# Strassen's scheme for probabilities times values in the attention of a Conformer block

## Chip, core and metric

The kernel runs on one core of one Trainium2 chip. The metric is the device time of one execution in microseconds; the time of a kernel is the median of several runs. A profiled execution is another, single execution with the hardware profiler on.

## What is computed

One Conformer block for 2 sequences of 4,000 tokens of 512 features (bf16): feed-forward with half a residual, attention with one head of 512 features, a convolution module with a norm over all tokens, a second feed-forward and a last layer norm.

```python
h = _layernorm(x)
x1 = x + 0.5 * (_silu(h @ w_ff1_a) @ w_ff1_b)          # 512 -> 2048 -> 512
h = _layernorm(x1)
q, k, v = h @ w_q, h @ w_k, h @ w_v
p = _softmax(einsum('btd,bsd->bts', q, k) * D ** -0.5)
x2 = x1 + einsum('bts,bsd->btd', p, v) @ w_o
h = _layernorm(x2) @ w_pw1                              # 512 -> 1024
h = h[..., :D] * _sigmoid(h[..., D:])
dc = depthwise convolution of h over 3 tokens, then a norm over all tokens
x3 = x2 + _silu(dc) @ w_pw2
h = _layernorm(x3)
return _layernorm(x3 + 0.5 * (_silu(h @ w_ff2_a) @ w_ff2_b))
```

## The kernel before

**Tiling.** The 8,000 tokens are cut into 16 chunks, 8 per sequence: seven of 508 tokens (four tiles of 127) and one of 444. Everything of one chunk is done by the four engines in a hand-written order of emission: `S.op` and `S.dma` put an instruction into the queue of its engine and work out its waits from the buffers that it reads and writes; each engine then goes through its own queue in order. `after(n, fn)` puts work off by n steps (a step, `tick`, is one key tile in attention), `lags` is a list of products held back. SyncE (SP) issues nearly all DMAs, one at a time in the order of emission, so a DMA that waits for its data holds all DMAs behind it.

**Stages.** Feed-forward one runs to about 410 us of the span, attention to about 1475, the end of the convolution with its norm to about 1503, feed-forward two and the last norm to the end. The work of the convolution module for chunk g-1 and g-2 is laid between the key tiles of attention chunk g. Both feed-forward stages already use Strassen's scheme in most chunks (`ff_quad`, L1006), whose weight sums are made by `ff_weights` and, for feed-forward two, by `wa_sums` (L982) in attention chunk 2 from weights (`raw`) that are loaded in chunk 1.

**Attention.** Weights are folded beforehand: `M` takes the place of w_q and w_k, `Wvo` that of w_v and w_o, so both scores and the second product work on the layer-normed tokens h themselves. For one sequence, `hT` holds h with features on the partitions (for the scores), `h` holds it with tokens on the partitions (`keys` in the profile). `attention` (L1276) goes through 16 query chunks g and, in each, through 32 key tiles kt: 31 of 128 keys and a tail of 32. For each key tile:

- scores: four matmuls (`s` <- `work`,`keys`, one per 128 features) into one of four PSUM banks;
- `act` (L663): ScalarE exponentiates into a ring of 8 tiles `P`;
- VectorE adds the tile in f32 to `acc` (L1312), the sums of the softmax;
- `values` (L1320), four tiles later: four matmuls (`y` <- `work`,`keys`) of h's four blocks of 128 features times `P`, accumulated over the whole chunk in four further banks `Yb`.

After the last key tile `split_sums` and `sums_by_query` (L1402, L1417) turn `acc` into a reciprocal per query, by a DMA transpose; `copy_o` (L1431) takes `Yb` out of PSUM by ScalarE and VectorE (L660), and `project` (L1437), in steps 6 to 9 of the next chunk, multiplies by `Wvo` and adds to the tokens (`residual`, L872). Then `projected` starts `ln_job` (L753): statistics (L726), four norms by VectorE (L745), and behind each a DMA transpose (L671) from SP, whose results feed the first convolution product, `conv_b` and `conv_a` (L1471, L1481), at key tiles 22 and 27 of the same and 3 and 8 of the following chunk; `taps_beside` (L1528) does the depthwise part on VectorE.

For the next chunk, `fetch_queries` (a DMA transpose from `keysd` in DRAM) is at key tiles 7 to 10 and `q_group`, four matmuls by `M` each, at 14, 16, 18 and 20 (in chunk 1 at 3, 4, 14, 16, with the fetch in chunk 0), with copies by ScalarE and VectorE in turn (L1222). Chunk 0 begins while feed-forward one's last chunk ends; SP then still loads most key tiles of the first sequence (`load_rest`). In chunks 7 and 8 the keys of the second sequence are loaded over those of the first, key tile by key tile (`key_tile`, L1392). Conv results go to DRAM and are fetched again by `fetch_conv` (L1574): pieces 0 to 2 at the end of attention, pieces 3 and 4 in the first steps of feed-forward two (hook at L1990), where `swish` (L1642) on ScalarE reads them.

If a bound on the scores fails (`fold_weights`, L1673, against `SCORE_LIMIT`), a second program with row maxima runs instead (`any_score`); with these inputs it does not.

Of the kernel before, what the change touches and what calls it, by code (L numbers as in the profile page):

```python
# [25 lines left out]
HALF = 64  # L26
HC, HD, HF = CHUNK // 2, D // 2, FC // 2
# [6 lines left out]
SCORE_LIMIT = 60.0  # L34
# [224 lines left out]
class Conformer:  # L259
    LN_SLOTS = 4  # L260

    TAIL_AT = 18
# [28 lines left out]
    def memory(self):  # L291
        nc = self.nc
        self.XR = Region(nc, "xt", (self.SLOTS + 1) * 4096)
        self.bxs = [[Buf("x%d.%d" % (n, t)) for t in range(TPC)] for n in range(self.SLOTS + 1)]
# [13 lines left out]
        self.raw = E.view(16384, DC * F).rearrange("p (c f) -> p c f", c=DC)  # L308
        self.b_raw = [E.buf("raw", 16384 + n * 4096, 4096) for n in range(DC)]
# [37 lines left out]
        def take(n):  # L347
# [23 lines left out]
        oWvo = take(4096)  # L371
        self.M = C.view(oM, 2048).rearrange("p (c f) -> p c f", c=DC)
# [7 lines left out]
        self.b_OTr = [Buf("OTr") for cc in range(DC)]  # L380

# [20 lines left out]
        GW = CHUNK + 4  # L402

# [22 lines left out]
        homes = ((C, oQ1), (E, 28672))  # L426
# [10 lines left out]
                   [(C, oOT + k * 1024) for k in range(4)] + [(E, k * 1024) for k in range(4)]),  # L437
# [104 lines left out]
    def slot(self, c, n=SLOTS):  # L542

        return self.SLOTS if c == TCB - 1 else self.SLOTS - n + (c - (c >= TCB)) % n
# [157 lines left out]
    def load_x(self, c):  # L702
        if c < NCK:
            self.place(c, self.slot(c))
# [48 lines left out]
    def ln_job(self, c, kind, eng="DVE", plan=(1, 1, 2, 2, 3, 4, 5, 5, 6, 6), slot=None, pe=None):  # L753
# [5 lines left out]
        def tile(ti):  # L759
            if kind == "key":  # L760
                self.ln_norm(c, sl, ti, self.h2[c % 2][ti][0:TILE, :], self.b_h2[c % 2][ti], eng)
# [85 lines left out]

    def store_keys(self, c):
# [7 lines left out]
        h2, b_h2 = self.h2[c % 2], self.b_h2[c % 2]  # L856
        put(self.pieces(c, flat, self.h2c[c % 2]), b_h2, [self.b_keysd[c]] + (self.b_keyst if c == TCB - 1 else []))
# [124 lines left out]
    def wa_sums(self, w, b_w, n):  # L982
# [7 lines left out]
        for h in range(2):  # L990
            self.S.op("DVE", lambda e, h=h: e.tensor_tensor(out=out[:, h], in0=x[:, h], in1=y[:, h], op=op),
                      reads=rd + b_w, writes=wr)

# [218 lines left out]
    def q_group(self, b, qc, dc):  # L1212
# [8 lines left out]
        if dc % 2:  # L1221
            self.S.op("DVE", lambda e: e.tensor_copy(self.qT[s][:, dc, 0:W], ps[:, 0:W]),  # L1222
                      reads=[b_ps], writes=[self.b_qT[s][dc]])
        else:
            self.act(self.qT[s][:, dc, 0:W], ps[:, 0:W], AF.Copy, [b_ps], [self.b_qT[s][dc]])
# [50 lines left out]
    def attention(self, old, hook, done):  # L1276
        S = self.S
        LAG = 4
        for g in range(NCK):
            b, qc = divmod(g, TCB)  # L1280
            s, W = qc % 2, width(g)
            if self.any_score:
                if qc == 0:
                    self.pop(len(self.lags))
                    if not b:
                        self.load_rest(2 * KT, KT * 2)
                    if b:
                        for kt in range(KT):
                            self.key_tile(1, kt)
                self.row_max(qc)  # L1290
            for kt in range(KT):
                kc, kj = divmod(kt, TPC)
# [3 lines left out]
                if kt < KT - 1:  # L1296
                    ps, b_ps = self.sbank()
                    p = self.nxt("Pa", self.NP - 1) if self.any_score else self.nxt("P", self.NP)
                    for cc in range(DC):
                        self.mm(ps[:, 0:W], self.hT[kc][:, kj, cc, :], self.qT[s][:, cc, 0:W],  # L1300
                                cc == 0, cc == DC - 1 and not self.any_score,
                                [self.b_hT[kc][kj], self.b_qT[s][cc]], b_ps)
                    if self.any_score:
                        self.mm(ps[:, 0:W], self.one3, self.m3[:, 0:W], False, True,
                                [self.b_one3] + self.b_m3, b_ps)
# [776 lines left out]
```

## Time and profile before

| | us |
|---|---|
| median of 3 runs (1947.73 to 1954.67) | 1950.62 |
| the profiled execution | 1952.81 |
| its span | 1948.8 |
| PE, DVE, ACT busy in the span | 1934.8, 1426.1, 1003.0 |
| PE, DVE, ACT busy from 60 to 450 us | 388.1, 312.8, 274.1 |
| from one chunk of attention to the next (518.0 to 585.9) | 67.9 |

The span lies within the profiled execution's own time; the difference of 4 us is before its first and after its last instruction. The span's lines in the profile are named by engine: PE is TensorE (PEld its weight loads), DVE VectorE, ACT ScalarE, POOL GpSimd, SP the engine that issues DMAs (SPq its queue). A group is written as line, engine, operation, output <- inputs by tile name, shapes, count, busy time, mean of one, idle time before it and what ended that. Matmuls overlap in the record: a busy PE need not be at its peak, so a matmul's price is read from the distance of two starts.

### The profile page before, as it was taken

How to read it: one execution, taken by the hardware profiler on the slowest of the kernel's cores; microseconds unless marked ns; L12 is line 12 of the kernel's file. 1: busy time of each engine (PE TensorE's matmuls, PEld its weight loads, DVE VectorE, ACT ScalarE, POOL GpSimd, SP SyncE). 2: the span in 40 equal slices, each digit the busy share in tenths (PEclk: the TensorE clock that was granted, in tenths of full speed). 3: DMA queues.
4: the chain of work that ended last, by engine and by line, in shares of the span. 5: the costliest groups of instructions: out<-in, count | busy, mean ns of one | idle time of the engine just before them, and what ended most of it. 6: DMA issues, size and time to landing. Idle time of an engine off the chain costs nothing.

```text
span 1948.8 us, 31991 instructions
## 1 busy us (share of the span) xinstructions
PE 1934.8 (99%) x12626; PEld 1258.4 (65%) x12626; DVE 1426.1 (73%) x2743; ACT 1003.0 (51%) x1726; POOL 108.4 (6%) x235
## 2 busy tenths in 40 slices
PE   9999999999999999999999999999999999999998
PEld 5899999954444444445444444444455789999997
DVE  7788888745566667666766666676687888888885
ACT  5677777743333333333333333333337678777774
POOL 1000000000000000000000000000002000000000
PEclk9999999999999999999999999999999999999999
DMA  8233344264121221114531212211134322222211
GB/s 183 72 87 86 80 114 106 69 159 133 26 52 25 49 53 49 37 44 101 135 61 41 59 28 47 55 49 35 44 108 127 75 76 65 78 53 55 63 40 44
DMA packets 270443, 139.59 MB, mean 72 GB/s; under 512 B 202568, under 2 KB 261643, under 8 KB 270287
## 3 DMA queue, kind: packets, MB, share of 16 engines
q1 hardware_dynamic: 269609, 137.14, 28.4%
q8 instruction: 101, 1.65, 0.3%
q14 instruction: 55, 0.45, 0.1%
q10 hardware_dynamic: 678, 0.34, 0.1%
HBM read 53.26 MB, written 39.20 MB: 47 GB/s over the span
## 4 chain that ended last, share of the span: by engine, by line
PE 95%; SPq 2%; DVE 1%; DMA 1%; issue 0%; ACT 0%; POOL 0%; POOLq 0%; DVEq 0%
PE y L613 48%; PE s L613 47%; SPq L671 1%; SPq L667 1%; DVE work L726 0%; SPq L706 0%; DMA work<-in_dw_dram 0%; DMA work<-keysd 0%; DMA work<-work 0%; DVE xt L872 0%; SPq L675 0%; DVE work L905 0%; DVE xt L745 0%; PE y L641 0%; DVE sums L1003 0%
## 5 line engine op out<-in xcount | busy, mean ns | idle before, releaser
L613 PE MATMUL y<-work,keys 128*127 128x256 bf16 (+2 forms) x3904 | 739.9, 324 | 0.0
L663 ACT ACTIVATE work<-s 128x508 bf16<-128x508 f32 (+2 forms) x543 | 317.9, 586 | 642.8 <-PE s L613 640.4
L613 PEld LDWEIGHTS y<-work,keys 128*128 128x128 bf16 (+1 forms) x3904 | 408.2, 117 | 232.1 <-DVE work L660 0.6
L1312 DVE TENSOR_TENSOR work<-work 128x508 f32<-128x508 f32 (+1 forms) x480 | 324.1, 675 | 260.7 <-ACT work L663 257.9
L613 PE MATMUL s<-work,keys 128*128 128x508 bf16 (+2 forms) x2240 | 506.0, 356 | 0.0
L613 PEld LDWEIGHTS s<-work,keys 128*128 128x128 bf16 (+1 forms) x2240 | 195.7, 97 | 228.7 <-ACT work L663 5.8
L663 ACT ACTIVATE keys<-s 128x508 bf16<-128x508 f32 (+1 forms) x281 | 163.7, 585 | 176.8 <-PE s L613 114.7
L613 PE MATMUL y<-wff,keys 128*127 128x256 bf16 (+3 forms) x1592 | 210.0, 281 | 0.2 <-DVE xt L959 0.2
L726 DVE BATCH_NORM_STATS2 work<-xt 127x6 f32<-127x512 bf16 x311 | 196.5, 680 | 3.5 <-DMA xt<-in_x_dram 3.4
L613 PE MATMUL s<-sums 128*128 128x254 bf16 x1296 | 194.4, 273 | 2.2 <-DVE s L1038 2.2
L613 PE MATMUL s<-work,wff 128*128 128x508 bf16 (+4 forms) x884 | 188.5, 353 | 0.7 <-ACT work L663 0.4
L613 PEld LDWEIGHTS y<-wff,keys 128*127 128x127 bf16 (+1 forms) x1592 | 176.7, 136 | 18.1 <-issue 7.1
L918 DVE TENSOR_TENSOR keys<-keys 128x1016 bf16<-128x1016 bf16 x240 | 160.2, 680 | 4.2 <-ACT keys L663 2.1
L613 PE MATMUL s<-work 128*127 128x512 bf16 (+4 forms) x569 | 143.7, 378 | 5.2 <-DMA work<-in_dw_dram 2.1
L613 PEld LDWEIGHTS s<-sums 128*128 128x128 bf16 x1296 | 126.8, 98 | 20.5 <-DVE s L1038 2.4
L733 POOL TENSOR_TENSOR work<-work 127x4 f32<-127x4 f32 (+1 forms) x76 | 77.2, 1015 | 1046.8 <-DVE work L731 1046.8
L613 PE MATMUL y<-work,wff 128*128 128x254 bf16 (+1 forms) x892 | 135.3, 274 | 0.0
L613 PEld LDWEIGHTS s<-work,wff 128*128 128x128 bf16 x884 | 81.1, 98 | 81.5 <-issue 4.9
L663 ACT ACTIVATE work<-xt,work 127x512 bf16<-127x512 bf16 x148 | 119.6, 810 | 17.2 <-DVE work L738 16.9
L613 PEld LDWEIGHTS s<-work 128*127 128x127 bf16 (+2 forms) x569 | 66.3, 119 | 63.0 <-issue 3.4
L1038 DVE TENSOR_TENSOR s<-s,sums 128x508 f32<-128x508 f32 x108 | 74.9, 693 | 34.0 <-PE s L613 21.2
L613 PEld LDWEIGHTS y<-work,wff 128*128 128x128 bf16 x892 | 87.0, 98 | 10.4 <-ACT keys L663 0.5
(130 smaller groups left out, 1607.7 us busy)
## 6 DMA issues: line engine op xcount, KB each, us to landing
xd<-xt SPq DMA_DIRECT2D x28, 448.0 KB, 3.0
xt<-xd SPq DMA_DIRECT2D x28, 448.0 KB, 3.6
keys<-keysd SPq DMA_DIRECT2D x62, 128.0 KB, 2.3
out_dram<-xt SPq DMA_DIRECT2D x14, 448.0 KB, 3.2
dcvd<-wff SPq DMA_DIRECT2D x48, 127.0 KB, 1.8
keys<-dcvd SPq DMA_DIRECT2D x12, 508.0 KB, 3.7
xt<-in_x_dram SPq DMA_DIRECT2D x13, 448.0 KB, 4.6
wff<-in_w_ff_b_dram SPq DMA_DIRECT2D x8, 512.0 KB, 7.7
```

The costliest lines, as they stand in the source:

```text
L613: self.S.op("PE", lambda e: e.matmul(out, lhsT, rhs, start=start, stop=stop, **kw), reads=reads, writes=[bank], inc=stop if inc is None el ...
L663: return self.S.op("ACT", lambda e: e.activation(out, in_, func, **kw), reads=reads, writes=writes)
L667: return self.S.dma(eng, k, lambda e: e.dma_start(dst, src), reads=reads, writes=writes)
L671: return self.S.dma("SP", k, lambda e: e.dma_start_transpose(dst, src), reads=reads, writes=writes)
L726: self.S.op("DVE", lambda e: e.bn_stats(self.st[sl][:, ti, 0:6], x), reads=[b_x], writes=[self.b_st[sl][ti]])
L733: S.op("POOL", lambda e: e.tensor_tensor(out=self.rs[sl][:, 0:n], in0=self.mv[sl][:, 0:n, 1], in1=self.neghalf[0:TILE, 0:n], op=ALU.pow), ...
L918: self.S.op("DVE", lambda e, out=out, x=x, y=y, op=op: e.tensor_tensor(out=out, in0=x, in1=y, op=op), reads=rd, writes=wr)
L1038: S.op("DVE", lambda e: e.tensor_tensor(out=out, in0=h[:, W], in1=m5, op=ALU.add), reads=[b_h, b_m5], writes=[b_out])
L1312: S.op("DVE", lambda e, p=p: e.tensor_tensor(out=acc, in0=acc, in1=self.P[p][:, 0:W], op=ALU.add), reads=[self.b_P[p], self.b_acc[s]], wri ...
```

## The change

In chunks 0 to 14 the product of probabilities and values of key tiles 0 to 29 goes by pairs of key tiles in Winograd's form of Strassen's scheme: with a pair's 256 keys as two halves, the queries as two halves of 254, and the features as two halves of 256, seven products of half width (two matmuls each) stand in place of eight matmuls of full width. Tile 30 and the tail stay plain, and so does chunk 15.

- `exp_pair` writes each exponential as two pieces into two rings (`R`, `T`); `pair_sums` makes five sums and differences in bf16 and adds two of them to `acc`, on VectorE; where 31 tiles were added in f32, one operation per pair and one for tile 30 are left.
- `pv`: products 1, 2, 5, 6, 7 run from key tile 7 on, each in a PSUM bank of its own; products 3 and 4 and the last pairs' remainder run in key tiles 0 to 6 of the next chunk, in banks that `pv_join` has emptied; scores have three banks in place of four. `pv_join` puts the seven together with six operations on VectorE and three on ScalarE.
- The forms of h that the scheme needs (three sums kept beside h in `VF`, two differences in place) are made by VectorE: for the first sequence in chunk 0 (`v_here`), for the second ahead, in chunks 0 and 1, through DRAM (`v_ahead`), and loaded in chunks 7 and 8 (`v_back`). Chunk 15 loads 30 plain key tiles again at key tiles 7 to 14.
- All query copies and the four norms of `ln_job` before the convolution go to ScalarE; the projection moves to key tiles 9 to 12, the norms to 16 and 17, convolution pairs to 20 and 24 and, in the next chunk, 3 and 14; the query fetch moves from key tile 7 to 9, the tail's scores from 18 to 22.
- The weight sums of feed-forward two are made in the last chunk of feed-forward one (`wa_ahead`, through DRAM), and read again at the first step of feed-forward two (`wa_back`), ahead of `fetch_conv(3)`.
- `SCORE_LIMIT` falls from 60 to 1.5; the first program is still the one that runs.

The core of the diff (moved buffers, joins, forms and the fallback's copy of the old loop are left out):

```diff
+PAIRS = 15
-SCORE_LIMIT = 60.0
+SCORE_LIMIT = 1.5
-    TAIL_AT = 18
+    TAIL_AT = 22
...
+    def exp_pair(self, g, kt, ps, b_ps):
+        i, odd = divmod(kt, 2)
+        n, m, _, _ = self.p_home(g, i)
+        W, hw = width(g), width(g) // 2
+        oTo, oR, oTe = self.offs
+        lo, hi = ((oR + n * 4 * HC, oTe + m * 2 * HC), (oTo + m * 2 * HC, oR + n * 4 * HC + 2 * HC))[odd]
+        t = self.E.view(lo, hw)
+        out = bass.AP(tensor=t.tensor, offset=t.offset, ap=[list(t.ap[0]), [(hi - lo) // 2, 2], [1, hw]])
+        self.act(out, ps[:, 0:W].rearrange("p (h k) -> p h k", h=2), AF.Exp, [b_ps],
+                 [self.b_R[n] if not odd else self.b_R2[n], self.b_T[odd][m]], scale=SCALE)
+    def pair_sums(self, g, j, step):
+        S, s, W = self.S, g % TCB % 2, width(g)
+        hw = W // 2
+        i, n = 2 * j, min(2, PAIRS - 2 * j)
+        r, m, ft, b_f = self.p_home(g, i)
+        R = self.Rt[:, r:r + n, :, 0:hw]
+        a11, a22 = R[:, :, 0], R[:, :, 1]
+        te, to = [t[:, m:m + n, 0:hw] for t in self.Tt]
+        b_te, b_to = [b[m:m + n] for b in self.b_T]
+        b_11, b_22 = self.b_R[r:r + n], self.b_R2[r:r + n]
+        f = [ft[:, k, 0:n, 0:hw] for k in range(3)]
+        if step < 5:
+            out, x, y, op, rd, wr = ((f[0], a11, to, ALU.add, b_11 + b_to, [b_f[0]]),
+                                     (f[1], te, a22, ALU.add, b_te + b_22, [b_f[1]]),
+                                     (f[2], a11, a22, ALU.add, b_11 + b_22, [b_f[2]]),
+                                     (te, te, a11, ALU.subtract, b_te + b_11, b_te),
+                                     (to, to, a22, ALU.subtract, b_to + b_22, b_to))[step]
+            S.op("DVE", lambda e: e.tensor_tensor(out=out, in0=x, in1=y, op=op), reads=rd, writes=wr)
+            return
...
+    PV_BANK = {1: 4, 6: 5, 7: 6, 5: 7, 3: 7, 2: 3, 4: 3}
+    def pv(self, g, n, pairs):
+        hw = width(g) // 2
+        ps, b_ps = self.bank(self.PV_BANK[n])
+        for i in pairs:
+            r, m, ft, b_f = self.p_home(g, i)
+            R, T, f = self.Rt[:, r], [t[:, m] for t in self.Tt], ft[:, :, i % 2]
+            he, ho, v = self.h[2 * i], self.h[2 * i + 1], self.VF[i]
+            b_he, b_ho, b_v = self.b_h[2 * i], self.b_h[2 * i + 1], self.b_VF[i]
+            form, b_1, mv, b_2 = {1: (v[:, 0], b_v, f[:, 2], b_f[2]), 2: (he[:, 0:HD], b_he, f[:, 1], b_f[1]),
+                                  3: (he[:, HD:D], b_he, R[:, 0], self.b_R[r]), 4: (ho[:, 0:HD], b_ho, R[:, 1], self.b_R2[r]),
+                                  5: (ho[:, HD:D], b_ho, f[:, 0], b_f[0]), 6: (v[:, 1], b_v, T[0], self.b_T[0][m]),
+                                  7: (v[:, 2], b_v, T[1], self.b_T[1][m])}[n]
+            for u in range(2):
+                self.mm(ps[:, u * hw:(u + 1) * hw], form[:, u * 128:(u + 1) * 128], mv[:, 0:hw],
+                        i == 0 and u == 0 and n not in (3, 4), u == 1, [b_1, b_2], b_ps, skip_group_check=True)
...
+    def units(self, g, kt, fast, lag, group):
+        end = PAIRS // 2 - 1
+        if lag:
+            o = g - 1
+            if kt == 0:
+                self.pv(o, 1, group(end))
+                self.pv_rest(o, 0, (2, 5))
+                self.pv(o, 2, group(end + 1))
+                self.pv(o, 5, group(end + 1))
+                self.pv_rest(o, 1, (2, 5))
+                self.pv_join(o, 0)
+                self.split_sums(o)
+                self.sums_by_query(o % TCB % 2)
+            elif kt == 1:
+                for n in (6, 7):
+                    self.pv(o, n, group(end))
+                for n in (1, 6, 7):
+                    self.pv(o, n, group(end + 1))
+                self.pv_rest(o, 0, (7, 6))
+                self.pv_rest(o, 1, (7, 6))
+                self.pv_join(o, 1)
+                self.pv_join(o, 2)
+            elif kt < 7:
+                m = (kt - 2) * 6
+                for n in range(m, m + 6):
+                    self.pv(o, 3 if n >= PAIRS else 4, [n % PAIRS])
+                if kt == 2:
+                    self.pv_join(o, 3)
+                    self.pv_join(o, 4)
+                if kt == 4:
+                    self.pv_join(o, 5)
+                if kt == 6:
+                    self.pv_join(o, 6)
+            elif 9 <= kt < 9 + TPC:
+                self.project(o, kt - 9)
+        if not fast:
+            return
+        j, r = divmod(kt - 7, 4)
+        if 0 <= j <= end:
+            order = ((1, 6), (7,), (2,), (5,)) if j == 0 else ((2, 5), (1,), (6,), (7,))
+            for n in order[r]:
+                self.pv(g, n, group(j))
+        j, r = divmod(kt - 4, 4)
+        if 0 <= j <= end:
+            for n in ((0, 1), (2, 3, 4), (5,), (6,))[r]:
+                self.pair_sums(g, j, n)
+        if kt == KT - 2:
+            for n in (0, 1):
+                self.pair_sums(g, end + 1, n)
+        if kt == KT - 1:
+            for n in (2, 3, 4, 5):
+                self.pair_sums(g, end + 1, n)
+            self.sum_plain(g, KT - 2, self.P30, self.b_P30)
...
+    def keys_swap(self, g, kt, G):
+        at = g * KT + kt
+        if g == 0:
+            j, r = divmod(kt - 3, 3)
+            if 0 <= j <= G and r < 2:
+                for n in range(2 * r, 2 * r + 2):
+                    self.v_here(j, n)
+            if kt in (26, 27):
+                self.v_rest(kt - 26)
+        if g < 2:
+            for j, lo in enumerate((6, 12, 18, 24, 32, 35, 41, 44)):
+                if at in (lo, lo + 3, lo + 4, lo + 6):
+                    for n in {0: (0,), 3: (1, 2), 4: (3, 4), 6: (5,)}[at - lo]:
+                        self.v_ahead(j, n)
+        if TCB - 1 <= g <= TCB:
+            at -= (TCB - 1) * KT
+            for k in range(KT):
+                if (6 + k * (2 * KT - 12) // KT if k < KT - 1 else KT + 6) == at:
+                    self.key_queries(1, k)
+            for j in range(G + 1):
+                if at == min(4 * j + 13, KT + 3 + j - G):
+                    self.v_back(j, True)
+                if at == KT + 5 + j:
+                    self.v_back(j, False)
+            if at in (KT + 3, KT + 4):
+                self.key_values(1, KT - 2 + at - KT - 3)
+            if at in (KT + 14, KT + 15):
+                self.v_rest(at - KT - 14)
...
+    def wa_back(self):
+        dst = self.E.view(0, 8192).rearrange("p (m f) -> p m f", m=8)
+        for half in range(2):
+            n = HF * 128 // 2
+            self.load(dst[:, :, half * n:(half + 1) * n], self.wsd[half].rearrange("p (m f) -> p m f", m=8),
+                      self.b_wsum, reads=[self.b_wsd[half]])
...
+        here, there = ((22, 27), (3, 8)) if any_score else ((20, 24), (3, 14))
         def att_hook(g, kt):
             if g == 0 and kt == 8:
                 self.load(self.Wp1, i["w_pw1"].rearrange("(c p) f -> p c f", p=128), [self.b_Wp1])
-            if kt in (22, 27) and (0 <= g - 1 < tail or g - 1 == tail and (22, 27).index(kt) < self.KEEP):
-                pair(g - 1, (22, 27).index(kt))
-            if 0 <= g - 2 < tail and kt in (3, 8):
-                pair(g - 2, 2 + (3, 8).index(kt))
+            if kt in here and (0 <= g - 1 < tail or g - 1 == tail and here.index(kt) < self.KEEP):
+                pair(g - 1, here.index(kt))
+            if 0 <= g - 2 < tail and kt in there:
+                pair(g - 2, 2 + there.index(kt))
             if g == 0 and self.rest:
                 self.load_rest(FC + kt, 3)
-            if kt == 12:
-                self.get_x(g, self.slot(g, 3))
-            if g == 1 and kt < DC:
-                self.load(self.raw[:, kt, :], i["w_ff2_a"].rearrange("(c p) f -> p c f", p=128)[:, kt, :], [self.b_raw[kt]])
-            if g == 2 and kt in (2, 5, 12, 15):
-                self.wa_sums(self.raw, self.b_raw, (2, 5, 15, 12).index(kt))
+            if kt == (12 if any_score else 22):
+                self.get_x(g, self.slot(g, 0, 2))
+            if g and kt == 9 and not any_score:
+                self.ln_job(g - 1, "in", "ACT", (2, 3, 4, 5, 6, 7, 8, 8, 9, 9), slot=0)
+                self.after(7, lambda: self.put_x(g - 1))
             if g == NCK - 1:
                 if 8 <= kt < 20 and not any_score:
                     self.tap_matrix(kt - 8)
                 if kt in (22, 25, 28):
                     self.fetch_conv((kt - 22) // 3)
-                if kt in (2, 5, 8):
-                    self.get_x((kt - 2) // 3, self.slot((kt - 2) // 3))
+                if kt in (12, 15, 18):
+                    self.get_x(kt // 3 - 4, self.slot(kt // 3 - 4, 2))
...
+                if c == 0 and f == 0:
+                    self.wa_back()
                 if c == 0 and f < 2:
                     self.fetch_conv(3 + f)
```

More of the change, by code (lines that the diff above doesn't have):

```diff
@@ new lines, in keys_swap @@
+    def keys_swap(self, g, kt, G):
[26 more added lines that the diff above has]
+                self.v_rest(at - KT - 14)
+        if g == NCK - 1 and 7 <= kt < 15:
+            for k in range(4):
+                n = (kt - 7) * 4 + k
+                if n < KT - 2:
+                    self.key_values(1, n)
@@ L1849, in projected @@
             self.after(3, lambda: self.put_x(g))
-        self.attention(old, att_hook, projected)
+        (self.attention_any if any_score else self.attention)(old, att_hook, projected)
+        self.ring = list(range(4))
         if any_score:
```

365 lines of the change are left out of this document (293 added, 72 removed).

## The prediction

> **What bounds the kernel now.** First the page's busy times and its chain of waits.
>
> ```profile
> span 1948.8 us, 31991 instructions
> PE 1934.8 (99%) x12626; PEld 1258.4 (65%) x12626; DVE 1426.1 (73%) x2743; ACT 1003.0 (51%) x1726; POOL 108.4 (6%) x235
> PE 95%; SPq 2%; DVE 1%; DMA 1%; issue 0%; ACT 0%; POOL 0%; POOLq 0%; DVEq 0%
> ```
>
> TensorE works for 99% of the span and carries 95% of the chain. Then a table of windows by stage: 500 to 1440 us is attention, 1500 to 1900 the second feed-forward; the columns are length and then busy time of each engine with its instructions, the granted clock, DMA share, GB/s.
>
> ```profile
> 500.00:1440.00 940.00, 940.00 (x4685) 437.32 (x4684) 631.71 (x1117) 320.40 (x561) 29.67 (x122) 1.00 0.22 54
> 1500.00:1900.00 400.00, 397.68 (x3359) 352.70 (x3357) 342.87 (x686) 304.62 (x515) 28.64 (x29) 1.00 0.27 69
> 518.00:586.00 68.00, 68.00 (x335) 31.24 (x333) 41.47 (x72) 23.09 (x40) 1.41 (x5) 1.00 0.16 38
> ```
>
> In attention PE never rests; in one chunk (last row) VectorE has 26 us to spare. So matmul time taken out of attention shortens it, up to the next wait. The list of PE's waits has one of note there:
>
> ```profile
> PE s L613 <- DMA work<-keysd: 1.9, 1, 1.9
> ```
>
> **Part 1, the products.** Prices come from the timeline, by distances between starts, since the mean of a matmul (377 ns) holds its overlap.
>
> ```profile
> 645.02 1.02 PE L613 MATMUL s<-work 128*128 128x508 bf16 x4
> 645.88 1.02 PE L613 MATMUL s<-work,keys 128*128 128x508 bf16 x4
> 646.74 1.02 PE L613 MATMUL y<-work,keys 128*128 128x508 bf16 x4
> ...
> 1604.90 0.42 PEld L613 LDWEIGHTS s<-sums,wff 128*128 128x128 bf16 x4
> 1605.34 0.43 PEld L613 LDWEIGHTS y<-work,wff 128*128 128x128 bf16 x4
> 1605.78 0.43 PEld L613 LDWEIGHTS s<-sums 128*128 128x128 bf16 x4
> ```
>
> Four matmuls of 508 columns start 0.86 us before the next four: 215.4 ns each over a longer stretch. The second three rows are the weight loads of the feed-forward, whose matmuls have 254 columns: 0.435 us for four, 109 ns each, each with its own weight load. A pair of key tiles costs 8 x 215.4 = 1,723 ns before and 14 x 109 = 1,526 ns after: 197 ns less. Fifteen pairs give 2.96 us a chunk. Tile 30 goes from four full to eight half matmuls (+0.01), the 32-row tail from four to eight narrow-row ones, which I count as one more 109 ns slot (estimate): 2.84 us net. Fourteen wide chunks save 39.7; the 444-query one, with 188 ns against an estimated 95 ns, saves 15 x (8 x 188 - 14 x 95) = 2.6, less 0.12. Sum **-42.2 us**, if PE stays the bound. Its bounds: 107.7 ns a half matmul (half of 215.4) would give 4 us more; 116 ns would take 22 us back (rival 4).
>
> **Part 2, VectorE.** Removed per chunk: 16 of the 31 f32 sums at L1312 (683 ns: 10.9 us), two query copies (687), four norms (407), two output copies (679): 15.3 us. Added: 35 bf16 sums of two 254-column pieces and 5 of one, 6 joins out of PSUM. The nearest rows:
>
> ```profile
> L1312 DVE TENSOR_TENSOR work<-work 128x508 f32<-128x508 f32 x378 | 258.3, 683 | 206.6 <-ACT work L663 205.1
> L1003 DVE TENSOR_TENSOR sums<-work x54: 415/418/427, 52.2 to 1879.5; 128x512 bf16<-128x512 bf16 x54
> ```
>
> L1003 also adds bf16 in strided pieces: 418 ns (middle of min/median/max). That gives 35 x 0.42 + 5 x 0.29 (estimate) + 6 x 0.68 = 20.2 us; at the f32 duration (683) it would be 10 us more. I take 0.42, the row of the same type and length. VectorE goes from 41.5 to about 46.4 of the chunk's new 65.1 us: hidden behind PE. ScalarE gets two copies, four norms (810 ns each in the page's L663 row) and joins in place of output copies, from 23 to about 28 us: hidden.
>
> **Part 3, chunk 0.** Here the forms of 15 pairs of batch 0 are made by VectorE while it runs: 8 groups of four operations (three like L1003, one of 1,024 at 0.69): 1.95 us each, 15.6 us, and half of batch 1's, 7.8 us. With its pair sums and joins' f32 sums (35 x 0.42 + 1.5 + 14 x 0.69 = 25.8) and 5 to 10 us of layer norms and residuals that is 54 to 59 us, while PE needs only 45.7 (products 3 and 4 slip into chunk 1). And the fetch of the next queries, one transposing DMA, moves from key tile 7 to 9 in SP's queue:
>
> ```profile
> 433.92 3.24 SPq L671 DMA_TRANSPOSE work<-keysd  x1
> ...
> 438.78 0.43 SPq L667 DMA_DIRECT2D wff<-in_w_pw_dram  x1
> 439.21 1.03 PE L613 MATMUL s<-work 128*128 128x508 bf16 x4 [1.88 <-DMA work<-keysd]
> ```
>
> It landed 5.25 us after its issue and PE already waited 1.88 us for it. SP is the bottleneck of this stretch, and the fetch now stands behind some eight more issues (0.43 to 0.5 us each by these rows, the key loads of two more tiles and the first load of batch 1's values): issued about 437.4, landed about 442.7. PE reaches that query group earlier than before (437.3): by then it has run eleven tiles' products in the old form (11 x 0.862 = 9.5 us) and ten product slots in the new one (10 x 0.436 = 4.4): 432.2. It waits 10.5 us, 8.6 more than before; behind it stand all scores, so VectorE starves in that time and its 54 to 59 us then end some 4 us later still. **+12.6**, from 6 (fetch lands with the old distance) to 18 (VectorE wholly behind).
>
> By the Trainium skill ("TensorE: Matmul & The Clock Gate", section "HAM oscillation — how this bites in real kernels") a PE gap over about 3.4 us drops the clock to half for another such window, which speaks against a change that makes a 10 us gap. The trace has no gap over 2.2 us inside, and its granted clock is 1.00 in attention and 0.97 over the first 60 us, 1.8 us of clock missing at the start; by that rule the sum would be some 1.8 us higher, within the range of this part.
>
> **Part 4, conv at key tile 20.** The four norms of the previous chunk feed four transposing DMAs, and the conv projection needs all four.
>
> ```profile
> 641.95 0.73 DVE L745 TENSOR_SCALAR work<-xt,work 127x512 bf16<-127x512 bf16 x2
> 642.38 5.12 SPq L671 DMA_TRANSPOSE work<-work  x4
> 653.60 1.67 PE L613 MATMUL s<-work,wff 128*128 128x508 bf16 x7
> ```
>
> They are issued one after the other in 5.12 us, the last lands 2.5 us after its issue (median in the DMA rows): 648.7, 4.9 us ahead of the projection at 653.60. After the change the norms run on ScalarE at tiles 16 and 17, the projection at 20 instead of 22. From the start of tile 16's scores: 0.86 scores, 0.44 product, 0.86 query group, 0.2 to ScalarE, its copy (0.49 to the next start), norm 0.81: first norm 3.66, transposes issued at 3.7, 4.9, 6.2, 7.5, last landed 10.0. PE gets there at 5 x 0.862 scores + 6 x 0.436 products + 3 x 0.862 query groups = 9.51. Wait 0.5 us in each of 11 chunks: 5.9. In chunk 1 two query groups are missing from that stretch: 2.2; in 7 and 8 the key transposes of batch 1 stand between: 2.7 and 1.9; in 15, without query groups, 1.1. **+13.8**, from 0 (everything half a microsecond earlier, other cover in 1, 7, 8) to 25 (half a microsecond later in each of 15 chunks, and queues in 7 and 8 twice as long).
>
> **Part 5, the start of the second feed-forward.** The weight sums are now read back there by two 1 MB loads at the head of SP's queue, ahead of the fetch of conv piece 3, and the second waits for the landing of the first since both name the same tiles; SP's queue stands behind it.
>
> ```profile
> 1501.10 1.23 SPq L667 DMA_DIRECT2D keys<-dcvd  x1
> ...
> 1510.97 0.83 ACT L663 ACTIVATE work<-keys,work 128x508 bf16<-128x508 bf16 x1
> ```
>
> The fetch was issued at 1501.10 and first used at 1510.97. The DMA engines are full to 1508 at about 345 GB/s; 1 MB in place of 0.5 MB lands about 1509.8, then 1.5 MB more take 4.4 us and 2.5 us of latency, 3.7 of issue and sharing: about 1518. ScalarE is busy without a gap here, so the delay passes on: **+7** (3 to 9).
>
> **Small seams.** Chunk 15 reloads 30 key tiles' values through SP beside its products (+0.5), the key swap in chunk 8 (+1, 0 to 6), making the weight sums in the last chunk of feed-forward one: 16 operations of 0.42 = 6.7 us on VectorE, which has 77 us of 390 free there (0 to 2). **+1.5**.
>
> **Sum.** -42.2 + 12.6 + 13.8 + 7 + 1.5 = -7.3. The profiled execution took 1952.81 us (span 1948.8 and 4.0 around it), 2.2 above the median of 1950.62: 1945.5, or **1943** against the median.
>
> **Rivals.** (1) The seams hide: the transposes land in time and chunk 0 loses only 6: 1943 - 13.8 - 6.6 = **1923**. For it: part 4 rests on half a microsecond. Against it: the fetch in chunk 0 was late already. (2) Slower: the chain norm, four transposes, projection is later by 1.5 us more in 14 chunks, since ScalarE now runs queue, exponentials and norms in one order: +21, **1964**; it decides from 1.0 us more a chunk. For it: no step of that chain has slack; against it: ScalarE is half idle in attention. (3) Slower: two-piece bf16 sums run at the f32 rate: +10 us of VectorE in chunk 0, which it bounds, and 56 of 65 us busy in others, for which I allow 5: **1958**. L1003 speaks against. (4) It doesn't save: half matmuls with a load each at 116 ns in attention, 15 x 14 x 15 x 7 ns = 22 us: **1965**; the feed-forward's 109 ns, with a load each too, speaks against.
>
> **How the numbers follow.** Forecast 0.42 (its own range 1935 to 1951), rivals 0.26, 0.15, 0.09, 0.08. A measurement here tells 0.3%, 5.9 us, from no change: faster is below 1944.8, slower above 1956.5. Faster: 0.26 and somewhat over half of 0.42, 0.23, is 0.49; slower: 0.11 of rival 2, 0.09, 0.08 and 0.01 is 0.29; the same 0.22. The range 1920 to 1964 leaves out 0.05 below and some 0.12 above.
>
> **What would show it.** In the new profile the chunk period falls from 67.9 to about 65.6; PE's waits name the query transpose in chunk 0 (about 10 us), `work<-work` at the conv projection (about 14 in all) and the conv fetch or ScalarE near 1470 to 1480; PE's busy time falls by about 42; L1312 and pair sums show 683 and near 420 ns. It is wrong if PE's waits are under 10 us in all, if VectorE is what PE waits for in ordinary chunks, or if half matmuls start over 111 ns apart.

## The result and the profile after

The changed kernel takes 1964.1 us (median of 5 runs, 1960.7 to 1968.3) against 1952.47 for the one before (5 runs beside them): a ratio of 1.0062, 95% interval 1.0041 to 1.0083. It is slower; the forecast was 1943. The page's first lines and chain:

```profile
span 1960.2 us, 35217 instructions
PE 1908.7 (97%) x14096; PEld 1393.3 (71%) x14096; DVE 1490.4 (76%) x3162; ACT 1070.9 (55%) x1833; POOL 120.9 (6%) x235
PE 89%; SPq 3%; DMA 3%; DVE 2%; ACT 1%; issue 1%; POOL 0%; POOLq 0%; DVEq 0%
```

The work shrank: 26 us less of busy TensorE. But TensorE's share of the chain went from 95% to 89%, and queues, DMAs and VectorE took the rest. PE's list of waits (time, number, longest) shows where; before, it came to some 8 us in all. The first and the last line below belong to the convolution at key tile 20, the second to chunk 0, the third to the start of feed-forward two:

```profile
PE s L666 <- DMA work<-work: 12.5, 8, 3.5
PE s L666 <- DMA work<-keysd: 11.1, 1, 11.1
PE s L666 <- ACT keys L716: 5.4, 1, 5.4
PE s L666 <- ACT work L716: 3.8, 6, 0.8
```

The same windows as before, with one ordinary chunk in the last row:

```profile
500.00:1440.00 940.00, 922.63 (x6096) 567.95 (x6094) 674.34 (x1451) 384.12 (x661) 42.33 (x120) 1.00 0.25 62
1500.00:1900.00 400.00, 393.85 (x3280) 345.83 (x3279) 337.44 (x680) 301.75 (x509) 29.82 (x32) 0.99 0.29 76
725.90:792.20 66.30, 65.65 (x430) 40.16 (x430) 48.15 (x102) 27.61 (x48) 3.30 (x9) 1.00 0.19 47
```

In attention TensorE now rests 17 us of 940; VectorE, 48 of 66 us in a chunk, does not bound an ordinary one. To sort the difference, each matmul is priced by its width at full rate (109 ns for 254 columns, 215 for 508, others in proportion to the 215), and what the distance to the next start exceeds that is a loss, put down to the place where it stands. The prices add up to 1937.5 us before and 1894.3 after; the losses to 4.2 and 58.9. By place, in the two profiled spans (1948.8 and 1960.2):

| | forecast | measured |
|---|---|---|
| matmuls, with the tail | -42.2 | -37.0 (-43.2 by prices, tail +6.2) |
| convolution at key tile 20, 15 waits | +13.8 | +20.0 |
| chunk 0 (410 to 500 us: 18.6 lost against 1.1) | +12.6 | +17.5 |
| start of feed-forward two | +7 | +5.6 |
| the rest, by difference | +1.5 | +5.3 |
| sum | -7.3 | +11.4 |

### The profile page after: what moved, and what is told of

It reads as the page before. It is cut to its first block, busy times and chain, and to the rows that moved or that the text cites. A ratio compares the mean times of both kernels' runs of the same rounds, so it can differ in the third digit from the quotient of the medians.

```text
span 1960.2 us, 35217 instructions
## 1 busy us (share of the span) xinstructions
PE 1908.7 (97%) x14096; PEld 1393.3 (71%) x14096; DVE 1490.4 (76%) x3162; ACT 1070.9 (55%) x1833; POOL 120.9 (6%) x235
## 4 chain that ended last, share of the span: by engine, by line
PE 89%; SPq 3%; DMA 3%; DVE 2%; ACT 1%; issue 1%; POOL 0%; POOLq 0%; DVEq 0%
PE s L666 49%; PE y L666 39%; SPq L724 1%; SPq L720 1%; DMA work<-work 1%; ACT work L716 1%; DMA wff<-keysd 1%; DMA sums<-wsd 1%; DVE work L779 0%; SPq L759 0%; DMA keys<-dcvd 0%; DMA sums<-in_w_ff_a_dram 0%; DMA work<-in_dw_dram 0%; ACT sums L716 0%; DVE sums L1471 0%
## 5 line engine op out<-in xcount | busy, mean ns | idle before, releaser
L716 ACT ACTIVATE sums<-s 128x508 bf16<-128x508 f32 (+2 forms) x577 | 338.7, 588 | 453.4 <-PE s L666 437.8
L666 PE MATMUL s<-work,keys 128*128 128x508 bf16 (+3 forms) x2240 | 506.6, 357 | 2.7 <-ACT sums L716 2.7
L666 PE MATMUL y<-work,keys 128*127 128x256 bf16 x1920 | 244.8, 273 | 0.0
L1471 DVE TENSOR_TENSOR sums<-sums 128x508 bf16<-128x508 bf16 (+1 forms) x600 | 205.8, 397 | 34.9 <-ACT sums L716 34.3
L666 PEld LDWEIGHTS y<-work,keys 128*127 128x127 bf16 x1920 | 216.2, 137 | 5.3 <-DVE keys L977 0.3
L666 PE MATMUL s<-work,wff 128*128 128x508 bf16 (+4 forms) x884 | 189.2, 356 | 24.0 <-DMA work<-work 12.5
L716 ACT ACTIVATE work<-xt,work 127x512 bf16<-127x512 bf16 x208 | 164.7, 808 | 16.1 <-DVE work L791 15.8
L1899 DVE SCALAR_TENSOR_TENSOR wff<-wff,s 128x508 bf16<-128x508 f32 (+1 forms) x57 | 38.8, 681 | 148.5 <-PE s L666 146.8
L666 PE MATMUL y<-sums,keys 128*128 128x254 bf16 (+2 forms) x1024 | 150.5, 280 | 0.8 <-DMA keys<-keysd 0.8
L1480 DVE TENSOR_TENSOR work<-work,sums 128x508 f32<-128x508 f32 (+1 forms) x195 | 131.5, 674 | 1.1
```

The costliest lines, as they stand in the source:

```text
L666: self.S.op("PE", lambda e: e.matmul(out, lhsT, rhs, start=start, stop=stop, **kw), reads=reads, writes=[bank], inc=stop if inc is None el ...
L716: return self.S.op("ACT", lambda e: e.activation(out, in_, func, **kw), reads=reads, writes=writes)
L1471: S.op("DVE", lambda e: e.tensor_tensor(out=out, in0=x, in1=y, op=op), reads=rd, writes=wr)
L1480: S.op("DVE", lambda e: e.tensor_tensor(out=acc, in0=acc, in1=sig[step - 5], op=ALU.add), reads=b_f[0:2] + [self.b_acc[s]], writes=[self.b ...
L1899: self.S.op("DVE", lambda e: e.scalar_tensor_tensor(out=out, in0=th, scalar=1.0, in1=ps[:, 0:W], op0=ALU.add, op1=ALU.mult), reads=[b_ps, ...
```

## The experiments

All are edits of the changed kernel; times are medians, the ratio is to the kernel before on the same chip, in brackets the lowest and highest time and the 95% interval. The kernel before took 1952.47 us beside the changed kernel, 1953.96 beside e1 to e4 and 1954.76 to 1955.02 beside e5 to e10, so gains against the changed kernel (ratio 1.0062) are taken from the ratios, times 1952.5 us; by the intervals such a gain is known to about 5 us.

**The convolution's two pairs later, by two key tiles and by one.**

```diff
-        here, there = ((22, 27), (3, 8)) if any_score else ((20, 24), (3, 14))
+        here, there = ((22, 27), (3, 8)) if any_score else ((22, 25), (3, 14))
```

> Changed kernel with the first two convolution pairs at key tiles 22 and 25 instead of 20 and 24. Theory A: the 15 waits at the convolution projection (20.0 us by start distances: 0.8 in ordinary chunks, 2.6, 3.6 and 2.4 in chunks 1, 7 and 8) are only a matter of place; two tiles (some 3.3 us) later all but parts of a microsecond are gone, and the time falls by 16 to 20 us (1944 to 1948). Rival B: the pair at 25 pushes its taps on VectorE into the end of the chunk, where the last pair sums are needed at once; the wait reappears at key tiles 0 and 1 as a wait for L1471, and the gain is under 10 us.

1943.30 us (1942.97 to 1944.23), ratio 0.9950 (0.9934 to 0.9967): a gain of 21.9 us by the ratios (20.8 by the medians). Of the fifteen waits one of 1.0 us and one of 0.3 are left by the distances of starts, as the first theory said:

```profile
PE s L666 <- DMA work<-keysd: 10.8, 1, 10.8
PE s L666 <- ACT keys L716: 6.1, 1, 6.1
PE s L666 <- ACT sums L716: 3.2, 3, 2.0
...
PE s L666 <- DMA work<-work: 0.8, 1, 0.8
```

`work<-work` fell from 12.5 to 0.8 and `ACT work` from 3.8 to 0.4, and nothing came in their place; an ordinary chunk takes 65.50 us in place of 66.27 (67.88 before). The waits are 18.7 us shorter; two stretches at half clock behind the waits in chunks 1 and 7 (last section) went with them, 1.7 us each. The change's place for these pairs, not its amount of work, cost 20 us, and with those two numbers changed the scheme is faster than the kernel before.

**Chunk 0: two waits over one another.** First the query fetch alone, then the forms of batch 1 alone, then both.

```diff
-                self.next_queries(g, kt, 9)
+                self.next_queries(g, kt, 2 if g == 0 else 9)      # e1, e6
-            for j, lo in enumerate((6, 12, 18, 24, 32, 35, 41, 44)):
+            for j, lo in enumerate((14, 17, 23, 26, 32, 35, 41, 44)):   # e5, e6
```

> Changed kernel with the query fetch of chunk 0 at key tile 2 instead of 9. Theory A: the 11.3 us wait of TensorE for work<-keysd is what chunk 0 loses; it goes, no other takes its place, and the time falls by 8 to 10 us against the changed kernel (about 1955). Rival B: VectorE, which stood 7.6 us until the load of batch 1's values landed (wff<-keysd, 437.2) with the pair sums behind it in its queue, is the next bound; TensorE then waits for sums from L1471 and the gain is 2 to 6 us (1958 to 1962).

1963.89 us (1960.5 to 1965.89), ratio 1.0053 (1.0035 to 1.0072): 1.8 us by the ratios, which is no gain clear of noise; in the profile 410 to 500 us loses 18.8 us, as before this edit (18.6). The wait for `work<-keysd` went and this one came, with one of 4.3 us for an exponential behind it:

```profile
PE s L666 <- DVE sums L1471: 8.8, 1, 8.8
```

VectorE's timeline in the same run shows why: an operation on the values of batch 1, which nothing needs before chunk 8, stood 10.93 us for its load, and the pair sums (L1471) that TensorE needed next stood behind it in the queue.

```profile
440.78 1.15 DVE L1558 TENSOR_TENSOR wff<-wff 128x512 bf16<-128x512 bf16 x2 [10.93 <-DMA wff<-keysd]
...
444.63 0.75 DVE L1471 TENSOR_TENSOR sums<-sums 128x508 bf16<-128x508 bf16 x2
```

> Changed kernel with the forms of batch 1 begun at key tile 14 instead of 6 (loads at 14, 17, 23, 26 of chunk 0 in place of 6, 12, 18, 24; those of chunk 1 as they were). Theory A (chunk 0 has two waits over one another, the query transpose that lands at 445.8 and VectorE's wait for the first load of batch 1's values, which ends at 437.2 and leaves VectorE behind): alone, the wait for the queries stays, shorter by the two DMAs that no longer stand ahead of it (8 to 11 us), VectorE's lag is smaller afterwards, gain 1 to 4 us. Rival B: only VectorE's wait counts, and the gain is 8 us or more.

1968.07 us (1966.87 to 1970.6), ratio 1.0068 (1.0051 to 1.0085): no gain. TensorE waited 10.8 us for the queries as before, and 4.3 us for pair sums at the start of chunk 1, where the forms now fall due. Both theories named a gain; the first got the wait right, but its gain did not come, and by the profile 410 to 500 us loses 22.2 us in place of 18.6.

> Both: the query fetch of chunk 0 at key tile 2 and the forms of batch 1 from key tile 14. Theory A (two waits over one another): only now does the chunk get shorter; TensorE's waits in it fall from 11.3 and 8.9 us to 2 to 5 in all, which is VectorE's own work (54 to 59 us against 46 of TensorE's), and the time falls by 6 to 10 us against the changed kernel (1954 to 1958). Rival B: VectorE's work by itself, not the loads, sets the length of chunk 0, and the wait only moves to later key tiles of chunks 0 and 1: gain under 3 us.

1960.23 us (1957.86 to 1962.13), ratio 1.0029 (1.0016 to 1.0042): a gain of 6.4 us by the ratios, at the low end of the first theory; in the profile 410 to 500 us loses 12.9 us in place of 18.6. TensorE's two long waits in chunk 0 fell to 4.8 and 2.7 us, more than the 2 to 5 in all that were named. What was left was not only VectorE's work: VectorE still stood 6.35 us for a load of batch 1's values, until 450.29. Moving that load had moved the wait. This led to the last experiment below.

**The start of feed-forward two.** First the order alone, then the order and buffers by halves.

```diff
-                if c == 0 and f == 0:
-                    self.wa_back()
                 if c == 0 and f < 2:
                     self.fetch_conv(3 + f)
+                if c == 0 and f == 2:          # e3; in e7 f == 1
+                    self.wa_back()
...
-                      self.b_wsum, reads=[self.b_wsd[half]])
+                      [self.b_wh[half]], reads=[self.b_wsd[half]])    # e7: the pieces of that half only
```

> Changed kernel with the two 1 MB loads of the weight sums issued after the fetches of conv pieces 3 and 4 instead of before them. Theory A: the 5.6 us wait of TensorE at the start of feed-forward two is the order of SP's queue; it goes, and the time falls by 4 to 6 us. Rival B: the loads, moved behind, hold up the transposes for chunk 1 or the sums that chunk 1 needs, and 2 us or more of it come back as waits for work<-work or for the weight sums.

1964.57 us (1958.53 to 1965.74), ratio 1.0050 (1.0030 to 1.0069): no gain clear of noise. The 5.6 us wait is gone, but TensorE waits 2.5 us for L1091, the sums that VectorE makes of the transposed tokens of chunk 1, and 2.2 for L1126, a wait that the kernel before had too (2.2 us, there L1038) and that the 5.6 us had cut to 0.6. SP's queue shows the rival's reason, in length of issue:

```profile
1509.31 10.91 SPq L720 DMA_DIRECT2D sums<-wsd  x2
1520.28 1.35 SPq L724 DMA_TRANSPOSE work<-work  x1
```

The pair of loads holds the queue for 10.91 us (10.73 in the changed kernel), the second waiting for the first, and the transpose for chunk 1 stands behind it.

> Changed kernel with the two loads of the weight sums behind the fetches of conv pieces 3 and 4, as in the third experiment, and with buffers named by halves, so that the second load no longer waits for the landing of the first. Theory A (what came back there was SP's queue standing behind that wait, with the transposes of chunk 1 in it): the 5.6 us wait goes and at most 1.5 us come back; gain 4 to 6 us. Rival B (the loads themselves are late for chunk 1, or their traffic is): waits of 2 us or more for sums stay near the end of chunk 0 of feed-forward two.

1962.2 us (1959.48 to 1967.02), ratio 1.0038 (1.0023 to 1.0053). By the ratios the gain is 4.7 us, as the first theory said, though the times alone do not settle it. In the trace the pair holds SP for 4.31 us in place of e3's 10.91; the wait of 5.6 us and that for L1091 are gone, and what is left is the wait of 2.2 us for the same operation as before (here L1127). Between the start of feed-forward two and its second chunk TensorE's waits take 2.9 us in place of the changed kernel's 6.3, and the stretch at half clock behind the 5.6 us, 1.7 us more, is gone too.

**The tail in one group.**

```diff
-                self.pv_rest(o, 1, (2, 5))
+                self.pv_rest(o, 1, (2, 5, 7, 6))
...
-                self.pv_rest(o, 1, (7, 6))
```

> Changed kernel with the eight 32-row matmuls of the tail in one group of four products at key tile 0, instead of two groups of two at key tiles 0 and 1. Theory A: four row strips of the array work at once and a group of four takes no longer than a group of two, and one change between full and 32-row matmuls (some 0.2 us by start distances) goes: about 0.3 us less in each of 14 chunks, 4 us in all, a chunk period of 65.9 in place of 66.3. Rival B: the eight take the same time together, and nothing moves (under 1 us).

1962.71 us (1959.47 to 1966.49), ratio 1.0047 (1.0031 to 1.0063): 2.9 us by the ratios, within noise of the 4 forecast. The trace settles it: an ordinary chunk takes 65.85 us, 0.42 less, as the first theory said. In the profiled execution (1965.54 us) 410 to 500 us lost 23.9 us in place of 18.6, with a wait of 5.1 us for L1471, which hides the gain there. The timeline of the changed kernel shows the piece: two groups of four 32-row matmuls, each followed by a full one.

```profile
1209.89 0.28 PE L666 MATMUL s<-wff,keys 32*128 32x254 bf16 x1
1209.89 0.28 PE L666 MATMUL y<-wff,keys 32*128 32x254 bf16 x1
1210.00 0.27 PE L666 MATMUL s<-wff,keys 32*128 32x254 bf16 x1
1210.01 0.27 PE L666 MATMUL y<-wff,keys 32*128 32x254 bf16 x1
1210.21 1.03 PE L666 MATMUL s<-work,keys 128*128 128x508 bf16 x4
...
1213.13 0.39 PE L666 MATMUL y<-wff,sums 32*128 32x254 bf16 x4
1213.45 1.03 PE L666 MATMUL s<-work,keys 128*128 128x508 bf16 x4
```

Two of them start together (1209.89, twice), then two more 0.11 us later; from the first to the next full matmul it is 0.32 us each time. Some 0.1 us passes ahead of a group as well, so that one costs 0.42 us; e4's group of eight costs 0.42 too. The kernel before has the same 0.32 us once, for four matmuls of twice the width:

```profile
1213.08 0.39 PE L613 MATMUL y<-wff,keys 32*128 32x508 bf16 x4
1213.40 1.90 PE L613 MATMUL s<-work,wff 128*128 128x508 bf16 x8
```

**Everything, and the forms spaced out.** e8 takes the five edits together (e7's form of the weight loads). In e9, besides, the forms of batch 1 whose loads are issued in chunk 0 are made seven key tiles after the load, and two of these four groups thereby move into chunk 1 (the old loop's lines are left out):

```diff
+            for j, plan in enumerate(((13, 20, 21, 22), (15, 22, 23, 24), (25, 32, 33, 34), (27, 34, 35, 36),
+                                      (37, 40, 41, 42), (39, 42, 43, 44), (45, 47, 48, 49), (46, 49, 50, 51))):
+                if at in plan:
+                    for n in ((0,), (1, 2), (3, 4), (5,))[plan.index(at)]:
+                        self.v_ahead(j, n)
```

> Everything at once: convolution pairs at 22 and 25, query fetch at 2 and forms of batch 1 from 14, weight sums split and behind the fetches, tail in one group. If the waits found are separate and nothing else takes their place, the gains add: 20.8 (convolution, measured) + 8 + 5 + 5 below the changed kernel: about 1925, 1.4% below the kernel before. If chunks 0 and 1 are bound by VectorE whatever the order, about 1935.

> As e8, with the forms of batch 1 made 7 key tiles after their load is issued in chunk 0 instead of 3 (loads at key tiles 13, 15, 25, 27, first operations at 20, 22 of chunk 0 and at 0 and 2 of chunk 1; the last four groups at 5 to 19 of chunk 1). Theory A: in e8 VectorE still stood 7.4 us (to 449.4) for the landing of such a load, with the pair sums behind it; without that wait the 5.3 and 2.5 us that TensorE waited for sums in chunk 0 go to under 2 in all, and the time falls by 5 to 7 us against e8. Rival B: VectorE's work alone is too long for chunk 0, the wait stays at 5 us or more near its end or at the start of chunk 1, and the gain is under 2 us.

> The kernel of e8 once more, on the same chip as e9, to compare the two: the ratio to the kernel before again 0.985 to 0.989.

e8: 1929.46 us (1927.37 to 1931.42), ratio 0.9869 (0.9852 to 0.9885), a gain of 37.7 us, between the two times named and nearer to the 1925. The same kernel again, e10: 1931.54 us, ratio 0.9879 (0.9861 to 0.9898), as expected. The gains of e2, e6, e7 and e4 add up to 35.9 us (21.9, 6.4, 4.7, 2.9), so these waits were separate. e9, beside e10: 1922.94 us (1920.0 to 1927.29), ratio 0.9844 (0.9825 to 0.9862), 7 to 9 us less than e10, a little over what the first theory gave; every run of e9 is below every run of e10. VectorE's list of waits in e8 has, for the loads of batch 1's values (time, number, longest):

```profile
DVE wff L1559 <- DMA wff<-keysd: 13.0, 2, 7.4
```

and in e9:

```profile
DVE wff L1559 <- DMA wff<-keysd: 4.7, 2, 2.7
```

TensorE waited 5.1 us for pair sums in chunk 0 of e8; in e9 no wait for them is over 0.8 us, and one of 2.8 us for an exponential is left. The windows below run from VectorE's first form to its last pair sum of chunk 0, in the changed kernel, e8 and e9; the busy time of VectorE is the third after the length:

```profile
419.66:481.34 61.68, 45.70 (x285) 25.73 (x284) 45.61 (x118) 23.30 (x41) 2.05 (x2) 0.92 0.73 211
420.69:477.17 56.48, 47.07 (x288) 26.63 (x287) 45.55 (x118) 23.05 (x40) 2.05 (x2) 0.91 0.73 214
419.42:465.75 46.33, 41.61 (x263) 24.03 (x262) 41.93 (x110) 22.52 (x39) 2.05 (x2) 0.96 0.80 228
```

VectorE's work there is 45.6 us, and in the first two it stands still for 16.1 and 10.9 us more. So what made chunk 0 long was the standing, most of it for loads of batch 1's values. Of e9's 10.2 us against e8, 6.5 are less standing and 3.6 are work moved into chunk 1; no run separates the two, and with VectorE busy for 41.9 of 46.3 us its work is now close to the bound. An ordinary chunk takes 65.07 us.

## Why the prediction was wrong

It named the places where time comes back, and the saving of the pairs. Four of its terms failed: the tail's price, the wait at key tile 20, the lag in chunk 0, and the clock behind waits, which it took as one piece of 1.8 us and left out of the sum.

**The matmuls: right.** 14 half matmuls start 109 ns apart; the forecast gave 2.84 us less a chunk, and e9, which has the tail in one group and no wait at key tile 20, has 67.88 - 65.07 = 2.81.

**The tail: mis-sized.** "Four to eight narrow-row ones, which I count as one more 109 ns slot" was the wrong price: the change also splits the group in two, and a group costs 0.42 us whether it holds eight or four of the new ones, with the change from full to 32-row matmuls and back in it. One group more in each of 15 chunks is 6.2 us where 1.6 were forecast.

**VectorE's durations: right; their sum: too high.** The row for strided pieces held, and rival 3 fell (groups by shape, in attention):

```profile
L1471 DVE TENSOR_TENSOR sums<-sums 128x508 bf16<-128x508 bf16 x450 | 162.3, 415 | 30.5 <-ACT sums L716 29.9
L1480 DVE TENSOR_TENSOR work<-work,sums 128x508 f32<-128x508 f32 x169 | 114.7, 679 | 1.0
```

The forecast took 420 and 683. But it added durations, and VectorE's overlap as TensorE's do: five pair sums at 426.82 take 1.76 us from the first start to the last end, so they start 0.34 us apart, not 0.42.

**Key tile 20: the mechanism right, the size low.** The chain came out as it was walked, and 0.2 us later at its end (timeline of the changed kernel, an ordinary chunk):

```profile
1247.86 1.51 ACT L716 ACTIVATE work<-xt,work 127x512 bf16<-127x512 bf16 x2
1248.69 5.13 SPq L724 DMA_TRANSPOSE work<-work  x4
...
1255.29 1.89 PE L666 MATMUL s<-work,wff 128*128 128x508 bf16 x8 [0.61 <-DMA work<-work]
```

Tile 16's scores started at 1245.02: norm at 2.84, forecast 2.85; transposes from 3.67, forecast 3.68; TensorE there at 9.5 and going on at 10.27, forecast 9.51 and 10.05 (9.51 and the wait of 0.54). A wait is a difference of two long chains, so 0.2 us on one made 0.78 of 0.54, and in chunks 1, 7 and 8 2.6, 3.6 and 2.4 of 2.2, 2.7 and 1.9. Chunks 3 and 10 waited 1.7 and 1.2 us, which is not explained. In all 20.0 in place of 13.8. The answer to "from half a microsecond earlier to half later" was thus in the upper half of its own range (0 to 25). Rival 2 had this place and the final time, 1964, but not the size: it needed 1.5 us more a chunk and got 0.25.

**Chunk 0: the wrong structure.** The step added a wait for the queries (8.6; measured 11.3 - 2.1 = 9.2) and a lag of VectorE after it (4; the rest of the 17.5 is 8.3, of which 1.9 is half clock behind the wait, 2.4 three short waits at 421 to 426 us, 3.3 two waits at 467 and 476). The runs show two waits side by side, each nearly as long as the other: TensorE's for the transposed queries and VectorE's for batch 1's values, both DMAs in the same busy stretch. VectorE's timeline of the changed kernel:

```profile
437.24 1.15 DVE L1558 TENSOR_TENSOR wff<-wff 128x512 bf16<-128x512 bf16 x2 [7.60 <-DMA wff<-keysd]
```

and SP's and TensorE's:

```profile
436.98 6.71 SPq L724 DMA_TRANSPOSE work<-keysd  x1
...
445.87 1.87 PE L666 MATMUL s<-work 128*128 128x508 bf16 x4 [11.11 <-DMA work<-keysd]
447.53 1.90 PE L666 MATMUL s<-work,keys 128*128 128x508 bf16 x4
```

Hence e1 and e5 gained nothing clear singly and e6 and e9 did. The forecast took VectorE's bound in chunk 0 as an amount of work, 54 to 59 us; the work is 45.6, and the bound was the order of its queue, with an operation on data not yet landed ahead of urgent ones. The issue was forecast at 437.4 and the landing at 442.7; the landing came 3 us later, since the old distance of 5.25 us became 8.8, but TensorE had come 2.4 us later too (434.6). That the wait was forecast so closely (10.5, measured 11.3) is thus in part luck.

**Feed-forward two: right** (5.6 for 7), and its reason too: the fetch issued at 1516.18, after both 1 MB loads, landed at 1522.7. The half clock behind this wait (1.7 us) is offset by the wait for L1038 before, which shrank by 1.6. That the order alone would not cure it (e3) was not in the forecast.

**The clock, and the rest** (5.3 for 1.5). The changed kernel loses 7.0 us in four stretches at half clock (last section): 1.9 in chunk 0, 1.7 each in chunks 1 and 7 and at the start of feed-forward two; the kernel before loses 1.8 in one. The 3.4 us of chunks 1 and 7 are most of what the rest has too much; 1.0 is a wait for the reloaded keys of chunk 15, and the remaining 0.9 is not taken apart. The prediction read the 1.8 us before as clock missing at the start; they stand at 36.6 to 40.0 us, right behind the gap that it named as the longest (2.3 us by distances of starts), so the trace before already showed what a wait can cost beyond its length.

The sum failed because it set some 44 us of saving, known to a microsecond, against losses known to a third of their size, and fell 18.7 us short on them: 6.2 at key tile 20, 5.2 at the matmuls with the tail, 4.9 in chunk 0, 3.8 in the rest, less 1.4 in feed-forward two. That was enough to turn a forecast gain into a loss. The range ended at 1964, 0.1 us short.

## What to carry to other kernels

When matmuls get shorter, everything timed by counting key tiles gets nearer: walk each chain (norm, transposes, product) in microseconds again, and where the margin is smaller than the error of the walk, put the consumer one or two steps later; here that was worth 20 of 42 us. An operation that works ahead belongs in an in-order queue only after its load has surely landed, or it holds back the urgent ones behind it. Where two waits lie side by side, taking one away shows nothing: take both. And a wait of TensorE can cost more than its length, by a stretch at half clock behind it.

## What the runs showed of the hardware

During the 11 us wait the granted clock fell to a half and stayed there for 4 us after it. Windows of the changed kernel around it, with the clock third from the end:

```profile
430.00:434.00 4.00, 4.00 (x28) 2.52 (x27) 0.00 (x0) 1.78 (x3) 0.00 (x0) 1.00 0.91 277
434.00:446.00 12.00, 0.89 (x7) 0.46 (x6) 8.56 (x20) 0.59 (x1) 0.00 (x0) 0.73 1.04 275
446.00:450.00 4.00, 4.00 (x13) 1.69 (x12) 1.04 (x3) 1.12 (x2) 0.00 (x0) 0.53 0.92 308
450.00:454.00 4.00, 4.00 (x26) 2.35 (x25) 3.20 (x8) 1.68 (x4) 0.00 (x0) 1.00 0.03 7
```

For these 4 us the clock is 0.53, and four matmuls of 508 columns take 447.53 - 445.87 = 1.66 us instead of 0.86; 13 matmuls ran where 26 to 28 do. That is about 2 us more for the wait. Much shorter waits did the same. These are the wait of 2.6 us in chunk 1 and the stretches behind it, and, in the last row, the one stretch of the kernel before:

```profile
521.90:524.40 2.50, 0.15 (x2) 0.00 (x0) 0.20 (x1) 0.35 (x1) 0.00 (x0) 1.00 0.55 136
524.90:528.20 3.30, 3.30 (x9) 1.19 (x8) 0.32 (x1) 0.59 (x1) 0.00 (x0) 0.50 0.12 42
528.30:531.60 3.30, 3.30 (x35) 1.83 (x34) 2.67 (x9) 1.46 (x3) 0.10 (x1) 1.00 0.05 10
36.70:40.00 3.30, 3.30 (x16) 2.27 (x14) 3.13 (x6) 0.59 (x1) 0.00 (x0) 0.50 0.09 17
```

The waits of 3.6 us in chunk 7 and 5.6 us at feed-forward two have such a stretch behind them as well (the clock is 0.50 from 924.3 to 927.6 and from 1524.9 to 1528.3), while those of 2.4 us in chunk 8 and 3.1 us at 35 us have none; what decides is not shown. A mean over a long window hides all this: the clock of 500 to 1440 us reads 1.00.

The place in the Trainium skill ("TensorE: Matmul & The Clock Gate", section "HAM oscillation — how this bites in real kernels") had announced the drop to half; its window of about 3.4 us agrees with the length of the shorter stretches here. As the least gap it does not hold in these traces, where 2.3 us (the kernel before) and 2.6 us were enough.

The other thing not expected: the DMA that transposes the queries took 6.71 us to issue and 8.8 to land, against 3.24 and 5.25 before. The share of the DMA engines does not tell the two apart: it is 1.06 from 434.0 to 439.2 us before, and 0.93 and 1.22 from 437.0 to 441.0 and 445.8 after. What differs is that a load of 1 MB (`wff<-in_w_pw_dram`, at key tile 8) is issued 2.1 us ahead of it, where it was 4.9 us behind it before. In e1, with the fetch ahead of that load again, it is 2.62 and 4.7 us; in e5, with the load of batch 1's values no longer ahead of it but the 1 MB load still there, 6.66 and 8.7. That points to the 1 MB load; no run moves that load alone.
